# New lists for the order of each engine's instructions in a linear attention and gated FFN kernel

## The chip, the cores and the metric

The kernel runs on one core of a Trainium2 chip. The metric is the device time of one execution in microseconds (us), the median of three runs. A smaller time is better. The engines are TensorE (PE), VectorE (DVE), ScalarE (ACT), GpSimd (POOL) and SyncE (SP); SP computes nothing here and issues every DMA of the kernel.

## The reference

Batch and heads are 8 each, the sequence has 576 positions, the head dimension is 64. The attention is linear; its output, with the heads side by side, is a matrix of 4608 tokens by 512, which goes through a gated feed-forward layer with 1536 inner columns.

```python
q_s = softmax over head_dim of q;  k_s = softmax over seq of k
kv  = np.einsum('bhsd,bhse->bhde', k_s, v)
x   = np.einsum('bhsd,bhde->bhse', q_s, kv)     # then 4608 x 512
a = x @ w_a;  b = x @ w_b                       # 512 x 1536 each
out = (a * b) @ w_out                           # 1536 x 512
```

The inputs are float32, the weights arrive as 64-bit words that the kernel turns into float32 itself.

## The kernel before

The 4608 tokens are worked off in nine chunks of 512. Chunk 0 is done in a start-up part while the weights are being converted; chunks 1 to 8 follow one loop. For each chunk there are six pairs of inner blocks. A pair needs seven products of an input operand (`xo`) with a combination of weights (`ws`), by a scheme with seven instead of eight block products; their results go to the PSUM tiles `kx`, `ky`, `ka` and `kp`. Every operand is kept as a high and a low part, and a product is 12 matmuls of 128x256 (`product`, L839). DVE and ACT combine the results, multiply a by b, and split the outcome into the parts `left`. From chunk 3 on the second layer is done by block products as well (`block_step`, L1478, tiles `po`): each item of six matmuls takes a `left` and a right operand, which is either held in SBUF (`kept`) or loaded (`xo<-dr`) into a ring of two `xo` tiles with two places each. In chunks 1 and 2 the second layer is plain (`project`, L859).

The weights' combinations don't fit in SBUF. They lie in DRAM (`dw`) and each is loaded again for every pair and chunk, 512 KB a time, into one of eight `ws` buffers (L482); the right operands come from `dr`, 256 KB a time (L1416). A load can be issued when the last matmul that reads the buffer's earlier content is done. The attention of the next chunk is spread between the pairs: keys and values are loaded (`kt`, `vt`), `kv_sums` (L588) multiplies them with weights of 64 columns into `pk`, ten matmuls for each pair of heads, and `x_product` (L770) makes the tile `px` from the turned queries. The queries' row statistics go to DRAM (`dq`) and come back spread over partitions (`mr<-dq`, L724, then DVE L731 and ACT L732).

The order of each engine's instructions isn't left to the scheduler. The table `ORDER` has, for each of the five engines, a list of places in the program's own order; `in_order` chains the instructions of that engine by it, and a program builds the semaphores from the data that they pass on. Each engine then works through its list strictly from front to back:

```python
for run in places.split():
    first, _, last = run.partition("-")
    chain += found[int(first):int(last or first) + 1]
for before, ins in zip(chain, chain[1:]):
    tc.add_manual_dep(ins, before.name, ...)
```

SP's list is at the same time the order of the DMA queue: a transfer that waits for its buffer holds up the issue of all that stand behind it.

Of the kernel before, what the change touches and what calls it, by code (L numbers as in the profile page):

```python
# [236 lines left out]
    ),  # L237
    "Pool": (
        "1 4 3 2 5-11 13 12 14 16 15 18 17 19 21 20 22-23 25-26 24 27-29 0 30 32 31 34 33 35 37 36 38-50 "
        "52-54 51 55-58 60-63 59 64-83 "  # L240
    ),
# [1504 lines left out]
```

## Time and profile before

| what | value |
|---|---|
| median of three runs | 957.57 us (955.74, 957.57, 962.2) |
| profiled execution | 960.79 us, its span 959.0 us |
| PE busy | 923.8 us, 96% of the span, 7109 records |
| DVE, ACT, POOL busy | 726.8, 482.1, 101.4 us |
| granted TensorE clock, mean | 0.999 |
| DMA | 308.50 MB, mean 322 GB/s |

The span runs from the first to the last instruction, and what lies around it is 1.8 us. A float32 matmul (L588 and the transposes) shows as two or more records. Matmuls overlap in PE: a record lasts longer than the distance to the next one's start, so a full PE is told by the distance of starts and not by busy time.

### The profile page before, as it was taken

Reading aid. Unit: us, or ns where it says so; the run is one execution under the profiler, and the core shown is the slowest. Engines: PE = TensorE matmul, PEld = TensorE weight load, DVE = VectorE, ACT = ScalarE, POOL = GpSimd, SP = SyncE. Lnnn points to the kernel's source line nnn. Section 1 sums busy time; section 2 is a strip of 40 time slices with the busy share of each in tenths; the row PEclk is TensorE's granted clock in tenths of the full one; section 3 lists DMA queues with packets and bytes.
Section 4 is the critical chain, followed back from the end, with each engine's and each line's share of the span. In section 5 each row is a group of like instructions: output and inputs, shape, how many; then the busy total and the mean of one; then the engine's idle time right before and its main releaser. Section 6 shows DMA issues by size and latency. Waiting matters only on the chain.

```text
span 959.0 us, 19492 instructions
## 1 busy us (share of the span) xinstructions
PE 923.8 (96%) x7109; PEld 846.1 (88%) x7109; DVE 726.8 (76%) x1572; ACT 482.1 (50%) x1346; POOL 101.4 (11%) x88
## 2 busy tenths in 40 slices
PE   6999999999999999989999999899999999999997
PEld 4666768988888999989999998899999999999996
DVE  7867879787897797669868886688868775876456
ACT  8968746433451446535645464345643564343331
POOL 1545351420000000000000000000000000000000
PEclk9999999999999999999999999999999999999999
DMA  9999889899999999998999899996999699957972
GB/s 356 366 384 413 327 296 344 308 325 356 341 405 330 322 384 346 341 302 330 334 319 346 315 329 341 272 384 231 326 319 378 229 364 296 367 184 262 356 255 83
DMA packets 126463, 308.50 MB, mean 322 GB/s; under 512 B 13600, under 2 KB 31648, under 8 KB 126368
## 3 DMA queue, kind: packets, MB, share of 16 engines
q1 hardware_dynamic: 126368, 307.25, 89.9%
q8 instruction: 57, 0.93, 0.4%
q14 instruction: 38, 0.31, 0.1%
HBM read 256.87 MB, written 48.23 MB: 318 GB/s over the span
## 4 chain that ended last, share of the span: by engine, by line
PE 63%; DMA 21%; SPq 3%; DVE 3%; ACT 2%; issue 2%; POOL 2%; DVEq 0%; POOLq 0%; ACTq 0%
PE kx L839 18%; PE po L1478 14%; PE ky L839 9%; PE ka L839 7%; DMA ws<-dw 5%; DMA mr<-dq 5%; DMA xo<-dr 5%; PE po L859 4%; PE pt L814 3%; PE kp L839 3%; PE pk L588 2%; PE po L849 2%; PE px L770 1%; DMA kt<-in_k 1%; SPq L724 1%
## 5 line engine op out<-in xcount | busy, mean ns | idle before, releaser
L839 PE MATMUL kx<-xo,ws 128*128 128x256 f32 x2016 | 277.1, 283 | 4.2 <-DMA ws<-dw 2.9
L839 PEld LDWEIGHTS kx<-xo,ws 128*128 128x128 f32 x2016 | 254.8, 188 | 9.2 <-issue 3.9
L1431 ACT CAST left<-cc 128x256 fp32r<-128x256 f32 x245 | 92.2, 404 | 110.7 <-DVE cc L1447 36.6
L839 PE MATMUL ky<-xo,ws 128*128 128x256 f32 x1008 | 138.8, 283 | 1.3 <-DMA ws<-dw 1.3
L1432 DVE TENSOR_TENSOR left<-cc,left 128x256 fp32r<-128x256 f32 x245 | 97.0, 419 | 46.4 <-ACT left L1431 45.3
L839 PEld LDWEIGHTS ky<-xo,ws 128*128 128x128 f32 x1008 | 127.9, 188 | 3.0 <-issue 1.6
L1478 PE MATMUL po<-xo,left 128*128 128x256 f32 x750 | 108.8, 284 | 6.1 <-DMA xo<-dr 5.4
L1478 PEld LDWEIGHTS po<-xo,left 128*128 128x128 f32 x750 | 96.8, 189 | 8.6 <-issue 4.7
L1478 PE MATMUL po<-kept,left 128*128 128x256 f32 x720 | 103.5, 283 | 0.2 <-ACT acc L1485 0.2
L839 PE MATMUL ka<-xo,ws 128*128 128x256 f32 x720 | 100.4, 283 | 2.3 <-DMA ws<-dw 2.1
L839 PEld LDWEIGHTS ka<-xo,ws 128*128 128x128 f32 x720 | 92.4, 188 | 4.6 <-issue 1.6
L1478 PEld LDWEIGHTS po<-kept,left 128*128 128x128 f32 x720 | 93.3, 189 | 1.5 <-ACT acc L1485 0.4
L681 ACT ACTIVATE qt<-qt,st 128x64 f32<-128x64 f32 x224 | 75.5, 339 | 17.5 <-DVE st L678 14.9
L814 PE MATMUL pt<-xo,ws 128*128 128x512 f32 x288 | 82.9, 427 | 1.1 <-ACT ga L821 1.1
L814 PEld LDWEIGHTS pt<-xo,ws 128*128 128x128 f32 x288 | 52.6, 188 | 23.2 <-issue 9.5
L518 POOL PARTITION_ALL_REDUCE mx<-m x20 | 15.1, 753 | 456.1 <-DVE m L529 443.9
L859 PE MATMUL po<-wo_w,gh 128*128 128x512 f32 x192 | 57.1, 397 | 0.3 <-ACT gh L350 0.3
L1447 DVE TENSOR_TENSOR cc<-cc 128x256 f32<-128x256 f32 x140 | 56.1, 419 | 1.6
L1630 DVE TENSOR_TENSOR cc<-ky,u 128x512 f32<-128x512 f32 x36 | 24.7, 687 | 26.7 <-ACT u L1629 24.4
L681 ACT ACTIVATION_READ_ACCUMULATOR qt<-qt,st 128x1 f32 x224 | 42.1, 188 | 0.0
L839 PE MATMUL kp<-xo,ws 128*128 128x256 f32 x288 | 40.5, 283 | 0.0
L381 POOL TENSOR_TENSOR wr<-raw,wr 128x512 int32<-128x512 int32 x24 | 34.6, 1444 | 55.6 <-DVE raw L378 33.9
(184 smaller groups left out, 1397.3 us busy)
## 6 DMA issues: line engine op xcount, KB each, us to landing
ws<-dw SPq DMA_DIRECT2D x277, 512.0 KB, 6.7
xo<-dr SPq DMA_DIRECT2D x125, 256.0 KB, 5.2
dw<-ws SPq DMA_DIRECT2D x42, 512.0 KB, 6.4
mr<-dq SPq DMA_DIRECT2D x112, 128.0 KB, 6.0
raw<-in_w_ab SPq DMA_DIRECT2D x24, 512.0 KB, 7.7
vt<-in_v SPq DMA_DIRECT2D x28, 325.0 KB, 6.4
qt<-in_q SPq DMA_DIRECT2D x32, 256.0 KB, 5.7
kt<-in_k SPq DMA_DIRECT2D x24, 320.0 KB, 5.8
```

The source lines that it names most:

```text
L381: nc.gpsimd.tensor_tensor(out=r, in0=u, in1=r, op=ALU.add)
L588: nc.tensor.matmul(pk[h * D:(h + 1) * D], kt[:, j, h], vt[:, j, h], start=(j == 0), stop=(j == J - 1),)
L681: nc.scalar.activation(out=qt[:, j, h], in_=qt[:, j, h], func=AF.Exp, bias=st[:, h, 0, j:j + 1], accum_out=st[:, h, 1, j:j + 1],)
L814: nc.tensor.matmul(pt, w[:, wp], x[g][:, xp], start=(g == 0 and i == 0), stop=(g == NP - 1 and i == 2),)
L839: ins = nc.tensor.matmul(pt[:, n], w[:, n, wp, c], x[:, xp, c], start=(first and n == 0 and i == 0), stop=(i == 5), skip_group_check=True,)
L849: nc.tensor.matmul(po[t], g[:, t * P:(t + 1) * P], wo_first[f], start=(f == 0), stop=(f == NF - 1),)
L859: nc.tensor.matmul(po[t], a[:, ts], wo[f][:, w], start=(f == 0 and i == 0), stop=(f == NF - 1 and i == 2),)
L1431: nc.scalar.copy(out=a[:, 0], in_=cc[:, n, part])
L1432: nc.vector.tensor_tensor(out=a[:, 1], in0=cc[:, n, part], in1=a[:, 0].bitcast(F32), op=ALU.subtract)
L1447: nc.vector.tensor_tensor(out=o, in0=x, in1=y, op=op)
L1478: nc.tensor.matmul(pt[:, t], x.left[:, ap, t * P:(t + 1) * P], w[:, wp], start=(first and t == 0 and n == 0), stop=(n == 2), skip_group_ch ...
L1630: nc.vector.tensor_tensor(out=cc[:, 3], in0=ky, in1=u4, op=ALU.add)
```

## The change

Only the table `ORDER` is changed: all five lists are replaced. The instructions themselves, their operands and their buffers are the same; the new table is seven lines longer, so every line number below it grows by 7 (L839 becomes L846, L588 becomes L595, L482 becomes L489). The words given with the change are that the lists come from a longer search that counts mean landing times and changes of weight width. Two lines of the diff, the starts of PE's list:

```diff
-        "4 0-3 5-15 30-33 16-29 34-42 44-47 43 49 60-63 50-55 48 56-59 80-82 64-73 86-89 74-76 90-91 "
+        "0-9 30-33 20-29 10-19 38-41 34-37 42-43 60-63 48 44-47 50-59 49 80-82 64-76 86-89 83-85 90 "
```

The first place is PE where chunk 2 passes into chunk 3. `pk` is the sum of keys times values with weights of 64 columns, `ka`, `kx` and `ky` are first-layer products, `po` belongs to the second layer. Before:

```order
L839 MATMUL kx_4146<-xo_3961,ws_4266 128x256 x12
L588 MATMUL pk_4347<-vt_4157,kt_4155 64x65 x6
L839 MATMUL ka_4436<-xo_4018,ws_4564 128x256 x6
L859 MATMUL po3_3009<-wo11_w_1425,gl1_4142 128x512
L588 MATMUL pk_4347<-vt_4157,kt_4155 64x65 x4
L588 MATMUL pk_4347<-vt_4161,kt_4159 64x65 x6
L839 MATMUL kx_4146<-xo_4025,ws_4378 128x256 x12
L588 MATMUL pk_4347<-vt_4161,kt_4159 64x65 x4
L839 MATMUL ky_4147<-xo_4021,ws_4394 128x256 x6
```

After, the second half of the same `pk`:

```order
L866 MATMUL po1_3007<-wo11_w_1425,gl1_4142 128x512
L866 MATMUL po3_3009<-wo11_w_1425,gl1_4142 128x512
L846 MATMUL kx_4146<-xo_4025,ws_4378 128x256 x12
L595 MATMUL pk_4347<-vt_4161,kt_4159 64x65 x10
L846 MATMUL ky_4147<-xo_4021,ws_4394 128x256 x6
L846 MATMUL kx_4434<-xo_3949,ws_4461 128x256 x12
L846 MATMUL ky_4147<-xo_4021,ws_4394 128x256 x6
```

The ten matmuls of each pair of heads stood in two pieces each, and now stand as one; in PE's whole list the runs of L588's matmuls go from 42 to 28, their 320 matmuls are the same. The first half of this `pk` now stands 25 rows further forward.

The second place is SP's list in chunk 5, ahead of the load `ws_7726`; `mr` are the statistics of the queries, `xo` right operands, `out` a store of results. Before:

```order
L724 DMA mr0_7443<-dq6_7274 64x1x512
L1416 DMA xo_4328<-dr12_3508 128x512
L1416 DMA xo_4328<-dr04_3279 128x512
L1416 DMA xo_4329<-dr21_3705 128x512
L724 DMA mr0_7443<-dq6_7274 64x1x512
L1416 DMA xo_4329<-dr22_3707 128x512
L724 DMA mr1_7444<-dq6_7274 64x1x512
L724 DMA mr0_7449<-dq6_7274 64x1x512
L1463 DMA out_0<-acc_6264 128x2x256
L724 DMA mr0_7449<-dq6_7274 64x1x512
L482 DMA ws_7726<-dw31_2265 128x1024
L482 DMA ws_7760<-dw34_830 128x1024
```

After:

```order
L1470 DMA out_0<-acc_6264 128x2x256
L731 DMA mr1_7450<-dq6_7274 64x1x512
L489 DMA ws_7679<-dw30_816 128x1024
L489 DMA ws_7703<-dw33_2328 128x1024
L719 DMA qtt_7543<-in_q_late 128x512
L489 DMA ws_7726<-dw31_2265 128x1024
L489 DMA ws_7760<-dw34_830 128x1024
```

Between the load `ws_7703`, which stood two rows above the first piece, and `ws_7726` there were eleven transfers, and now there is one; the right operands and most of the statistics have moved ahead of or behind the row of weights.

## Rows read from the trace of the kernel before

**Rows 1.** Page, part 3: DMA queue; packets, MB, share of 16 engines.
```profile
q1 hardware_dynamic: 126368, 307.25, 89.9%
```

**Rows 2.** Windows: us, busy time (instructions) by engine, PEclk, DMA share, GB/s.
```profile
400.00:440.00 40.00, 37.19 (x305) 36.23 (x304) 27.26 (x59) 14.78 (x32) 0.00 (x0) 1.00 1.00 332
...
560.00:640.00 80.00, 73.94 (x646) 71.33 (x645) 57.65 (x134) 37.17 (x112) 1.43 (x2) 1.00 0.97 334
...
840.00:880.00 40.00, 40.00 (x339) 39.98 (x338) 28.27 (x60) 14.60 (x34) 0.00 (x0) 1.00 0.59 209
...
sum 959.00, PE 923.78 PEld 846.12 DVE 726.75 ACT 482.11 POOL 101.35; mean PE 92.38 PEld 84.61 DVE 72.68 ACT 48.21 POOL 10.14
```

**Rows 3.** Waits of PE, whole span: us in total, times, longest.
```profile
PE po L1478 <- DMA xo<-dr: 5.4, 7, 1.5
PE pkb L1115 <- ACT kt_first L1109: 5.4, 1, 5.4
PE kx L839 <- DMA ws<-dw: 2.9, 2, 2.6
PE ka L839 <- DMA ws<-dw: 2.1, 2, 1.2
PE px L770 <- DVE xf L953: 1.8, 1, 1.8
PE px L770 <- ACT qh L350: 1.8, 1, 1.8
...
PE ky L839 <- DMA ws<-dw: 1.3, 1, 1.3
...
PE kx L839 <- ACT u L1564: 0.7, 1, 0.7
```

**Rows 4.** Timeline of PE, dense stretch: start us, us, engine, line, form, count.
```profile
841.78 1.59 PE L839 MATMUL kx<-xo,ws 128*128 128x256 f32 x12
843.21 0.88 PE L1478 MATMUL po<-xo,left 128*128 128x256 f32 x6
```

**Rows 5.** Timeline of PE at 363.6 to 370, around L588's weights of 64.
```profile
366.15 1.69 PE L839 MATMUL kx<-xo,ws 128*128 128x256 f32 x12
367.77 0.45 PE L588 MATMUL pk<-vt,kt 128*64 128x65 f32 x8
368.15 0.98 PE L839 MATMUL ky<-xo,ws 128*128 128x256 f32 x6
368.97 0.87 PE L1478 MATMUL po<-xo,left 128*128 128x256 f32 x6
```

**Rows 6.** Timeline of PE at 603 to 613; in brackets idle time before, releaser.
```profile
607.12 0.88 PE L1478 MATMUL po<-xo,left 128*128 128x256 f32 x6
610.62 1.67 PE L839 MATMUL kx<-xo,ws 128*128 128x256 f32 x12 [2.62 <-DMA ws<-dw]
```

**Rows 7.** Timeline of SP, the DMA queue's issuer, at 593 to 613.
```profile
593.72 6.08 SPq L1416 DMA_DIRECT2D xo<-dr  x3
...
603.53 1.12 SPq L482 DMA_DIRECT2D ws<-dw  x2
```

**Rows 8.** Page, part 6: DMA issues, count, KB each, median us to landing.
```profile
ws<-dw SPq DMA_DIRECT2D x277, 512.0 KB, 6.7
xo<-dr SPq DMA_DIRECT2D x125, 256.0 KB, 5.2
```

**Rows 9.** Chain that ended last, in order of time: start us, us, what.
```profile
228.41 6.86 DMA mr<-dq
...
810.00 5.68 DMA mr<-dq
```

**Rows 10.** Timeline of the end, 950 to 959, PE and DVE.
```profile
952.13 0.87 PE L1478 MATMUL po<-kept,left 128*128 128x256 f32 x6
...
953.66 0.69 DVE L1516 TENSOR_TENSOR acc<-acc 128x512 f32<-128x512 f32 x1
954.38 1.42 DVE L1688 TENSOR_TENSOR acc<-pl,acc 128x256 f32<-128x256 f32 x4
```

More of the change, by code (lines that the diff above doesn't have):

```diff
@@ L31 @@
     "PE": (
[89 rows of a table removed]
[96 rows of a table added]
     ),
     "Activation": (
[44 rows of a table removed]
[44 rows of a table added]
     ),
     "DVE": (
[68 rows of a table removed]
[69 rows of a table added]
     ),
     "Pool": (
-        "1 4 3 2 5-11 13 12 14 16 15 18 17 19 21 20 22-23 25-26 24 27-29 0 30 32 31 34 33 35 37 36 38-50 "
-        "52-54 51 55-58 60-63 59 64-83 "
+        "1 3 2 4-11 13-14 12 16-17 15 18-23 0 25 24 26-50 52-53 51 54-58 60-61 59 62-83 "
     ),
     "SP": (
[34 rows of a table removed]
[34 rows of a table added]
     ),
```

476 rows, old and new, of the table ORDER are left out of this document.

## The prediction

> **What bounds the kernel now.** I read the windows first. PE is busy in 923.78 of 959.00 us, DVE in 726.75, ACT in 482.11 [rows 2], so PE is the bound and what can be won is the time in which it stands still or works badly. Then the dense stretch: a matmul of 128x256 lasts 283 ns in the page, but twelve of them start at 841.78 and the next six at 843.21 [rows 4], so one takes 1.43 / 12 = 0.119 us of PE's time, and the end of a record lies 0.16 us behind the start of the next. So a wait costs about 0.16 us more than the idle time in front of it. From 840 to 880 PE has no idle time at all, and there the DMA engines are busy for 0.59; in 400 to 440 and 560 to 640, where PE is idle for 2.8 and 6.1 us, they are busy for 1.00 and 0.97 [rows 2]. PE loses time where the transfers are dense.
>
> Then the waits of PE, by releaser. Loads of `xo` and `ws` account for 5.4 + 2.9 + 2.1 + 1.3 = 11.7 us in twelve waits [rows 3]. Two waits of 1.8 us at `px` are put down to DVE and ACT, but the chain leads to the transfers of the queries' statistics, with 6.86 us issued at 228.41 and 5.68 us issued at 810.00 [rows 9]. With 0.16 for each of the fourteen waits that makes 11.7 + 3.6 + 2.2 = 17.5 us of waiting for transfers. The start-up takes 5.4 us before the first matmul [rows 3]. What is left of the idle time are some twenty shorter waits for ACT and DVE; the one of 0.7 us for `u` stands for them [rows 3].
>
> **The change, term by term.** No instruction is added or removed, so every term is a wait or a turn of PE that appears or goes.
>
> *Fewer changes of weight width.* The matmuls of L588 have weights of 64 columns, all their neighbours 128. In [rows 5], twelve matmuls of `kx` that stand behind one such run and ahead of another take 367.77 - 366.15 = 1.62 us in place of 1.43, which is 0.19 for going into one run and coming out of one; the six of `ky` that follow a run take 368.97 - 368.15 = 0.82 in place of 0.71, so 0.11 of it is the coming out. The last record of a run may also hold PE longer than those inside it: the eight records take 0.38 us, which would be at most another 0.12 for the run's end. One run costs 0.19 to 0.31 us, and I take 0.25, the middle. The lists have 42 runs before and 28 after, so 14 x 0.25 = 3.5 us go (2.7 to 4.3). Nothing hides this: it is PE's own time, in the engine that bounds.
>
> The Trainium skill, "TensorEngine Tiling (Array Packing)", Key Properties, says that a change of the tiling mode drains TensorE. By that rule each change would cost what one matmul has left when the next would start, 0.16 us by [rows 4], two a run, so 14 x 2 x 0.16 = 4.5 us in place of 3.5, and the forecast would be 947.7. The row, with 0.19 and more for a run, agrees that it costs, and lies a little below the rule.
>
> *Loads that come in time.* For each load of `ws` and `xo` behind the start-up I counted in the lists how much PE work lies between the last matmul that must be done before SP can issue it (through its own buffer, or through one that stands ahead of it in SP's list) and its first reader, at 0.119 us a matmul of 256 columns and in proportion for others. A load takes 6.7 or 5.2 us to land [rows 8], so leads below some 9 us are the tight ones. Before, 18 of `ws` and 23 of `xo` are below 9 us, and 5 and 12 of these below 7; after, 8 and 19, and 0 and 9. Setting the waits of the trace beside the leads of before, the 18 short ones of `ws` hold 5.3 us of the idle time, the 23 of `xo` 3.9, and the other 336 loads the remaining 2.5 to 3. In proportion to the counts, 5.3 x 8 / 18 = 2.4 and 3.9 x 19 / 23 = 3.2 stay, so 3.6 us go, and with 0.16 for five waits fewer 4.4.
>
> The longest of these waits shows what is meant. PE stops for 2.62 us ahead of 610.62 for a load of `ws` [rows 6], which SP issued at 603.53, after having stood for 6.08 us at three loads of `xo` from 593.72 on [rows 7]. In the list before, eleven transfers lie between the load `ws_7703` and this one, after it one; its lead goes from 7.7 to 9.0 us, and that of the next late one, `ws_7843`, from 8.4 to 15.3. For the statistics, the leads in front of the second place of `px` grow from 12 to 16 us to 17 to 22, but those at the first stay at 5.3 for one of two tiles. I let one of the two waits go, 1.8 + 0.16 = 2.0. Together 6.4 us go. The bounds: nothing goes, since the DMA engines have as much to move as before; or all but a fifth of the 17.5 goes, 14 us.
>
> *New tight handovers.* The new lists have 17 places at which only one group of matmuls (up to 1.35 us of work) stands between a product and a reader that needs the result of DVE or ACT, and the old ones 12. The one of which the wait is in [rows 3] is 0.7 us (`kx` for `u`). Five more at half of that, with 0.16 on top, cost 5 x 0.5 = 2.5; some of them sit where the other engine is free, so I take 1.5 (0 to 3). Here DVE's and ACT's next casts are queued behind the late one, and PE's next six or twelve matmuls wait.
>
> *The end and the start.* After its last six matmuls, which start at 952.13, DVE still does one sum over 512 columns and four over 256, up to 955.80 [rows 10]. In the new list nine matmuls of L1682 stand behind the last `po`, so the copy and the sum by ACT and DVE lie beside them, while DVE has one more short sum to do: 0.5 us go (0 to 1). In the start-up ACT does eight short exponentials before the second `kt_first` where it did six, but a transpose of the queries moves forward into the gap; I put it at 0 (1.5 either way).
>
> **Sum.** -3.5 - 6.4 + 1.5 - 0.5 = -8.9 us. The profiled execution took 960.79, its span and 1.8 us around it, and is 3.2 above the median of 957.57. The sum is the same for both: 951.9 for a profiled one, and against the median 957.57 - 8.9 = 948.7.
>
> **Rivals.**
>
> *The waits nearly all go.* If the landing times that the lists count with are those of the chip, most short leads are safe, also the many between 7 and 9 us. Then 14 in place of 6.4 go: 957.57 - 16.5 = 941.1. For it speaks that no `ws` lead is below 7 us any more; against it that nine `xo` leads still are, where the load takes 5.2 at the median and some longer.
>
> *The transfers are the bound in the dense stretches.* The bytes stay the same, 307.25 MB at 89.9% of all sixteen engines [rows 1], and where PE waits they are at 0.97 to 1.00 [rows 2]. Then a load that is issued sooner also lands slower, the other loads move back, and what PE wins at L588 in such a stretch it waits for the next load. Only the width in the rest of the span and the end remain, about 4 us: 953.5. Against it speaks that the stretch from 840 to 880 has room [rows 2], and that in the old list the load at 610.62 was late by its place and not by its 7 us of landing. The Trainium skill, "Perfetto Trace Analysis", What "DMA-bound" means, calls a kernel bound by DMA when the sixteen engines are. By that rule this case would hold through most of the span, as the shares bear out in those two windows alone.
>
> *Slower: SP's list stands still.* SP issues in order, and a transfer moved forward that waits for its buffer holds all that follow. The trace has this once at full size: 6.08 us for three issues [rows 7], and behind it waits of 2.62 [rows 6] and 1.3 [rows 3] at `ws`, 4.2 us with what the idle time leaves out. If the new list has such a place at four more of the chunks from 3 on, 16.8 us come, the 6.4 don't go, and the rest is -2.5: 957.57 - 2.5 + 16.8 = 971.9. It decides from one such place on (4.2 against 2.5). For it speaks that loads of `ws` now stand in rows of three and four with right operands behind them; against it that the count of leads takes in every row ahead in SP's list and still comes out longer.
>
> **How the numbers follow.** About 1% (9.6 us, so 948.0 and 967.1) is what a measurement of this kernel tells from no change; the three runs lie within 0.7%. The forecast has a chance of 0.5, and with the bounds of its terms it runs from 945 to 953, a little under half of it below 948.0. The first rival has 0.2, the second 0.2, the third 0.1, of which 0.07 is above 967.1. Faster by over 1%: 0.23 + 0.2 = 0.43. Slower by over 1%: 0.07. Within: 0.5. The range goes from 940 to 957; it leaves out the third rival and the lower part of the first.
>
> **What would show it.** In the trace after, twelve matmuls beside a run of L595 should still take 1.62 us, and there should be 28 runs. PE's waits for `xo` and `ws` should fall from 11.7 us to about 7.5, and those with `ws` should be the ones that go; the wait at `kx_7660` should be under 1 us. New short waits for DVE or ACT should add up to one or two us. If waits for transfers stay near 12 us at other places, the second rival has it; if SP shows several stops of 4 us and more ahead of waits at `ws`, the third. The forecast is wrong if the leads don't decide which loads are late, so that a count of them says nothing.

## The result and the profile after

The kernel after takes 936.26 us (median of four runs, 933.51 to 936.7), the kernel before 959.26 in the same set (955.74 to 962.2). The ratio is 0.9756, with a 95% interval of 0.9714 to 0.9797; a second set gave 934.95 us and 0.9732 (0.9706 to 0.9758). The change makes the kernel 2.4% faster. The forecast was 948.7 with a range from 940 to 957, so the time lies below the range.

The page of the profiled execution (936.7 us, span 934.9): busy time by engine, the DMA queue, and the shares of the chain that ended last.

```profile
PE 912.5 (98%) x7109; PEld 843.2 (90%) x7109; DVE 724.4 (77%) x1572; ACT 479.7 (51%) x1346; POOL 102.8 (11%) x88
...
q1 hardware_dynamic: 126368, 307.25, 92.6%
...
PE 83%; DMA 9%; DVE 5%; SPq 1%; ACT 1%; issue 1%; DVEq 0%; ACTq 0%
```

The last of these lines on the page of the kernel before:

```profile
PE 63%; DMA 21%; SPq 3%; DVE 3%; ACT 2%; issue 2%; POOL 2%; DVEq 0%; POOLq 0%; ACTq 0%
```

The chain that ended last now leads through PE for 83% of the span and through transfers for 9%; before it was 63% and 21%. The same 307.25 MB are moved as in [rows 1], in less time. PE is idle for 934.9 - 912.5 = 22.4 us; before it was 959.0 - 923.78 = 35.2 [rows 2]. The same windows as in [rows 2]:

```profile
400.00:440.00 40.00, 40.00 (x339) 40.00 (x338) 32.30 (x69) 19.01 (x41) 0.76 (x1) 1.00 1.03 356
560.00:640.00 80.00, 78.03 (x674) 77.25 (x673) 63.07 (x151) 37.53 (x100) 2.19 (x3) 1.00 0.97 343
840.00:880.00 40.00, 40.00 (x340) 40.00 (x339) 24.63 (x54) 13.20 (x30) 0.00 (x0) 1.00 0.94 335
```

In 400 to 440 the DMA engines are as busy as before (1.03, that of before is 1.00), and PE, which stood for 2.8 us, doesn't stand at all. The waits of PE over the whole span, with us in total, times and longest, answer to [rows 3]:

```profile
PE pka L1122 <- ACT kt_first L1116: 7.8, 2, 5.6
PE ky L846 <- DVE cc L1605: 1.8, 1, 1.8
PE po L1485 <- DVE acc L1515: 1.5, 1, 1.5
PE kx L846 <- ACT u L1636: 1.5, 1, 1.5
...
PE po L1485 <- DMA xo<-dr: 0.9, 1, 0.9
PE kx L846 <- DMA ws<-dw: 0.5, 1, 0.5
PE ky L846 <- DMA ws<-dw: 0.5, 1, 0.5
```

Of twelve waits for loads with 11.7 us three with 1.9 are left. The second place of `px` waits for nothing any more (before 3.9 us in three waits, 1.8 + 1.8 of them in [rows 3]). The waits for DVE and ACT behind the start-up are 5.4 us in six, before 5.5 in thirteen. Only the start-up waits longer, 9.4 in place of 7.7 us.

DVE too had stood for transfers, which the prediction doesn't speak of. The view of the waits of DVE, the line of the sum with the queries' statistics, in the kernel before:

```profile
DVE qtt L731 <- DMA mr<-dq: 15.2, 8, 2.7
```

And in the kernel after:

```profile
DVE qtt L738 <- DMA mr<-dq: 1.6, 3, 0.7
```

The timeline of PE around a run of L595 in the kernel after answers to [rows 5]:

```profile
551.39 0.87 PE L1485 MATMUL po<-xo,left 128*128 128x256 f32 x6
552.19 0.80 PE L595 MATMUL pk<-vt,kt 128*64 128x65 f32 x20
552.92 1.70 PE L846 MATMUL kx<-xo,ws 128*128 128x256 f32 x12
554.46 1.60 PE L846 MATMUL ky<-xo,ws 128*128 128x256 f32 x12
```

Six matmuls of `po` ahead of the run take 0.80 in place of 0.71 us, and the twelve of `kx` behind it 554.46 - 552.92 = 1.54 in place of 1.43. So going in costs 0.09 us and coming out 0.11, and what is lost inside the run comes on top.

The timeline of SP at the place of [rows 7]:

```profile
593.90 0.33 SPq L1423 DMA_DIRECT2D xo<-dr  x1
595.13 4.04 SPq L731 DMA_DIRECT2D mr<-dq  x4
599.73 1.69 SPq L489 DMA_DIRECT2D ws<-dw  x2
```

Where three `xo` held SP for 6.08 us, one `xo` takes 0.33 and four loads of `mr` take 4.04, and two loads of `ws` are out by 601.42; the first ones of [rows 7] were issued at 603.53.

The end, PE and DVE, as in [rows 10]:

```profile
927.77 1.78 PE L1689 MATMUL pl<-xo 128*128 128x512 f32 x7
...
929.08 0.68 DVE L1523 TENSOR_TENSOR acc<-acc 128x512 f32<-128x512 f32 x1
929.68 1.74 DVE L1695 TENSOR_TENSOR acc<-pl,acc 128x256 f32<-128x256 f32 x5
```

From the start of PE's last matmul to the end of the span it was 6.29 us and is 5.77.

**Where the time went.** The distance from each PE start to the next, set against the dense rate (869.0 us in both traces), leaves an excess of 78.4 us before and 54.8 after. Distances in front of which PE waited for `ws` or `xo` hold 14.5 us of it before and 2.4 after (-12.1); those at the second place of `px` 4.4 and 0 (-4.4, with 0.16 for each wait); the other waits for DVE and ACT lose 1.2, the start-up gains 1.7. Distances without a wait at or beside a matmul of L588 hold 18.4 and 14.4 (-4.0). The rest is 3.6 us less. Most of it lies in distances that are over 0.1 us too long and yet show no wait: 199 of them with 37.2 us before, 165 with 33.4 after. What held PE there isn't shown. Together with the end (-0.5) that is the 24.1 us between the two profiled executions.

### The profile page after: what moved, and what is told of

Its sections match the earlier page's. It is cut to its first block, busy times and chain, and to the rows that moved or that the text cites. A ratio compares the mean times of both kernels' runs of the same rounds, so it can differ in the third digit from the quotient of the medians.

```text
span 934.9 us, 19502 instructions
## 1 busy us (share of the span) xinstructions
PE 912.5 (98%) x7109; PEld 843.2 (90%) x7109; DVE 724.4 (77%) x1572; ACT 479.7 (51%) x1346; POOL 102.8 (11%) x88
## 3 DMA queue, kind: packets, MB, share of 16 engines
q1 hardware_dynamic: 126368, 307.25, 92.6%
## 4 chain that ended last, share of the span: by engine, by line
PE 83%; DMA 9%; DVE 5%; SPq 1%; ACT 1%; issue 1%; DVEq 0%; ACTq 0%
PE kx L846 22%; PE po L1485 15%; PE ky L846 11%; PE ka L846 8%; PE pt L821 7%; PE po L866 7%; PE po L856 4%; PE kp L846 3%; DMA ws<-dw 3%; PE px L777 2%; PE pk L595 2%; DMA dq<-sst 1%; DMA mr<-dq 1%; DMA xo<-dr 1%; DMA dr<-xo 1%
## 5 line engine op out<-in xcount | busy, mean ns | idle before, releaser
L846 PE MATMUL kx<-xo,ws 128*128 128x256 f32 x2016 | 274.9, 283 | 2.0 <-ACT u L1636 1.5
L846 PEld LDWEIGHTS kx<-xo,ws 128*128 128x128 f32 x2016 | 254.8, 188 | 5.8 <-ACT u L1636 1.7
L846 PE MATMUL ky<-xo,ws 128*128 128x256 f32 x1008 | 139.2, 283 | 2.4 <-DVE cc L1605 1.8
L846 PEld LDWEIGHTS ky<-xo,ws 128*128 128x128 f32 x1008 | 128.0, 189 | 5.0 <-DVE cc L1605 3.1
L1485 PE MATMUL po<-xo,left 128*128 128x256 f32 x750 | 106.7, 282 | 2.6 <-DVE acc L1515 1.5
L1485 PE MATMUL po<-kept,left 128*128 128x256 f32 x720 | 101.1, 282 | 0.0
L846 PE MATMUL ka<-xo,ws 128*128 128x256 f32 x720 | 100.8, 283 | 0.0
L846 PEld LDWEIGHTS ka<-xo,ws 128*128 128x128 f32 x720 | 93.0, 188 | 2.6 <-issue 0.5
L1636 ACT COPY u<-kx 128x512 f32<-128x512 f32 x36 | 21.1, 587 | 65.2 <-PE kx L846 40.3
```

Source lines behind the costliest of these rows:

```text
L846: ins = nc.tensor.matmul(pt[:, n], w[:, n, wp, c], x[:, xp, c], start=(first and n == 0 and i == 0), stop=(i == 5), skip_group_check=True,)
L1485: nc.tensor.matmul(pt[:, t], x.left[:, ap, t * P:(t + 1) * P], w[:, wp], start=(first and t == 0 and n == 0), stop=(n == 2), skip_group_ch ...
L1636: nc.scalar.copy(out=u4, in_=kx)
```

## The experiments

In what follows "over after" and "below before" are differences of ratios, times 960 us; the kernel after counts with 0.9756 for a_pkmore and with 0.9744, the mean of its two sets, for a_late and a_dve. Diffs of lists show rows of the engine named.

### Weight width

**b_pk28**: the kernel before; in PE's list alone the pieces of a `pk` are joined where nothing hinders it, 30 runs in place of 42. One of the twelve places in the table:

```diff
-1994-1999 2093-2098 1993 2000-2009
+2093-2098 1993-2003
```

> The kernel before with PE's list changed at the runs of L588 alone: the pieces of each ten are brought together ahead of the last piece, 42 runs become 30. Theory one, a run costs 0.25 us of PE's own time (0.19 to 0.31): 12 x 0.25 = 3.0 us less (2.3 to 3.7). The rule that each change drains TensorE: 12 x 0.32 = 3.8 us less. Rival, that what PE wins there it waits for at the next load, since the loads set its pace: 0 to 1.5 us less, and the waits for xo and ws grow from 11.7 us to 13 or 14.

Measured: 959.4 us, ratio 0.9976 (0.9953 to 1.0), 2.3 us below before (0 to 4.5), so a gain is not told from none by the times alone. In its trace the distances at L588 lose 18.4 - 14.7 = 3.7 us, which is 0.31 a run; waits for DVE and ACT come back in part. So the width alone is the small part of the gain.

**a_pkmore**: the kernel after with 61 runs in place of 28, each `pk` cut into pieces between the products that follow it.

```diff
-1281-1300 1386-1391 1380-1385
+1281-1284 1291-1294 1386-1391 1295-1297 1285-1287 1380-1385
```

> The kernel after with the tens of L595 from chunk 2 on cut into two or three pieces by the neighbouring groups of six or twelve, 28 runs become 61; all else as in the kernel after (936.3). At 0.25 us a run (0.19 to 0.31): 33 x 0.25 = 8.3 us more (6.3 to 10.2), 944.6. By the rule of a drain at each change, 0.32 a run: 10.6 more, 946.9. Rival, that the runs' length and not their number costs: no change, 936.

Measured: 949.96 us, ratio 0.989 (0.9854 to 0.9927), 12.9 us over after. Its timeline of PE at one place:

```profile
569.94 0.45 PE L599 MATMUL pk<-vt,kt 128*64 128x65 f32 x6
570.31 0.98 PE L850 MATMUL kx<-xo,ws 128*128 128x256 f32 x6
571.23 0.45 PE L599 MATMUL pk<-vt,kt 128*64 128x65 f32 x8
571.61 0.98 PE L850 MATMUL kx<-xo,ws 128*128 128x256 f32 x6
```

Six matmuls of `kx` between two runs take 571.23 - 570.31 = 0.92 us in place of 0.71. Its span is 16.2 us longer than that of after, of which 3.3 are waits (seven more, 2.2 us of idle time); 12.9 / 33 = 0.39 us a run, if all that is left is the runs'. That is over the bounds of both prices, but the time has some 5 us of uncertainty either way.

### Are the transfers the bound?

**b_half**: the kernel before; each load of `ws` brings one half of the bytes, and the products use that half for both blocks of the output, so that half of the weights of each combination take no part. Lists and matmuls stay.

```diff
-        last_w["load"] = nc.sync.dma_start(out=w.bitcast(F32), in_=dw[i, op].bitcast(F32))
+        last_w["load"] = nc.sync.dma_start(out=w[:, 0].bitcast(F32), in_=dw[i, op][:, 0].bitcast(F32))
...
-                        pt[:, n], w[:, n, wp, c], x[:, xp, c],
+                        pt[:, n], w[:, 0, wp, c], x[:, xp, c],
```

> The kernel before with half the bytes in each load of ws (256 in place of 512 KB, the same number of transfers in the same order); the products use the first half of the weights' columns for both halves, so the second half of the inner columns is not computed from its own weights. Same instructions on PE. This is the time with hardly a late load. Theory one and two alike expect landing times of ws near 4 us and a time 13 to 18 us below before, 941 to 946, if landing is what makes the loads late. If SP's stops for PE, DVE and ACT alone are to blame, 6 us or less are won.

Measured: 941.01 us, ratio 0.9791 (0.975 to 0.9832), 20.1 us below before with the lists of before. Its page, the loads with KB and median landing:

```profile
ws<-dw SPq DMA_DIRECT2D x277, 256.0 KB, 4.4
xo<-dr SPq DMA_DIRECT2D x125, 256.0 KB, 3.8
...
mr<-dq SPq DMA_DIRECT2D x112, 128.0 KB, 4.7
```

All loads land sooner, also those whose size is the same (`xo` 3.8 in place of 5.2 [rows 8], `mr` 4.7 in place of 6.0). PE's waits for loads fall to 0.5 us, those at `px` to 0.9, and DVE's for `mr` to 1.5. So transfers of full size had cost the kernel before some 20 us; with some 4 us of width that is as much as the change brings. That it is the same time is shown only by the next run.

**a_half**: the same edit on the kernel after.

> The kernel after with half the bytes in each load of ws, as in b_half; the second half of the inner columns is not computed from its own weights. What transfers still cost the kernel after: its waits for xo and ws (1.9 us) and those for ACT and DVE that go back to a late transfer (2 to 3): 2 to 5 us less than the kernel after, 930 to 933. It then lies 8 to 11 us below b_half (941.0), which is the width (14 runs at 0.37, 5.2) and the rest of the new order. If transfers are as much in the way as before, 10 us or more.

Measured: 935.46 us, ratio 0.9734 (0.9703 to 0.9766), the same as the kernel after (0.9756 and 0.9732). No load is waited for. A quarter of the bytes can go and little or nothing is won, so the rate of the transfers doesn't bound the kernel after, which runs at 92.6% of the sixteen engines and at 1.03 in the window above. How little is less sure than the median says: the four executions take 928.86 us at a granted clock of 0.999, 934.09 at 0.997 and 936.84 and 936.9 at 0.993, so a few us for fewer bytes, as expected, aren't ruled out.

Taken together, the four kernels show what the lists do. With all the bytes the new lists bring 24.6 us (1 less 0.9744), with half of those of `ws` only 5.5 (0.9791 less 0.9734, some 5 either way). So about 19 us of the gain are there only while the loads are of full size: that part is time which late transfers cost, and what is left is about the width.

**a_cap6**: the kernel after; each transfer in SP's list waits in addition for the one six places ahead of it to land. By the program it waits for the one eight places ahead at 818 of 850, and in no trace are there more than eight on the way.

```diff
+    if engine == mybir.EngineType.SP:
+        for before, ins in zip(chain, chain[6:]):
+            tc.add_manual_dep(ins, before.name, ...)
```

> The kernel after, with each transfer made to wait for the landing of the one six places ahead of it in SP's list in place of eight; lists, bytes and all else the same. Theory one, the hold of SP by the transfer eight places ahead is what makes loads late: loads then issue later, the waits for xo and ws come back (1.9 us to 10 or more), and the time is 8 to 30 us longer than the kernel after. Theory two, the DMA engines' rate is the bound: six transfers in flight keep the sixteen engines as busy as eight, each lands sooner by the same share, and the time stays within 4 us of the kernel after.

Measured: 942.15 us, ratio 0.9809 (0.9779 to 0.984), 7.2 us over the kernel after in the same set (934.95). That lies between the two theories. The loads of `ws` land in 5.9 us in place of 6.4 (the line of its page is below), but SP stands longer for the landing of earlier ones; DVE's waits for `mr` rise from 1.6 to 10.2 us, PE's for DVE and ACT from 5.4 to 8.4.

```profile
ws<-dw SPq DMA_DIRECT2D x277, 512.0 KB, 5.9
```

### Mending the kernel before, one list at a time

**b_sp**: the kernel before; in SP's list 13 loads on which PE waited move one to eight rows forward. One of them:

```diff
 L1416 DMA xo_4328<-dr12_3508 128x512
+L482 DMA ws_7726<-dw31_2265 128x1024
 L1416 DMA xo_4328<-dr04_3279 128x512
...
 L724 DMA mr0_7449<-dq6_7274 64x1x512
-L482 DMA ws_7726<-dw31_2265 128x1024
```

> The kernel before with SP's list alone changed: 13 of the 16 loads of ws and xo that came late in its trace are moved ahead by 1 to 8 rows. They hold 11.9 us of PE's idle time, 14 with 0.16 for each. Theory one, place and delay of the issue decide: 8 to 12 us less, since some loads that are pushed back become late; 947 to 951, and the waits for xo and ws fall from 11.7 to 2 to 5 us. Theory two, the DMA engines are the bound in the dense stretches: a load that goes ahead makes another one late, within 3 us of the kernel before, and the waits stay at 9 to 13 us.

Measured: 954.61 us, ratio 0.9931 (0.9904 to 0.9958), 6.6 us below before, less than expected. Lines of PE's waits:

```profile
PE px L770 <- DVE xf L953: 2.3, 1, 2.3
...
PE px L770 <- ACT qh L350: 1.9, 1, 1.9
PE po L1478 <- DVE left L1432: 1.8, 1, 1.8
```

PE's waits for loads fall from 11.7 to 2.4 us, but those at `px` rise from 3.9 to 6.0 and those for DVE and ACT from 5.5 to 7.9.

**b_sp2**: the same idea with 35 rows of SP's list, none moved more than eight places.

```diff
+L474 DMA dw_1549<-ws 128x1024
 L474 DMA dw_1667<-ws 128x1024
 L491 DMA ws_y<-dy_700 128x512
 L491 DMA ws_y<-dy_712 128x512
-L474 DMA dw_1549<-ws 128x1024
```

> The kernel before with SP's list alone changed, further than in b_sp: 35 rows moved by up to eight places over the whole program, loads and statistics both, each where its issue, its landing and the rule of eight transfers in flight leave it time. PE's, DVE's, ACT's and POOL's lists are as before. If the gain of the kernel after lies in SP's list: 9 to 14 us less than the kernel before, PE's waits for xo, ws and at px from 15.3 to 5 or less. If SP's order is held by when PE's list frees the buffers, and PE's own list must change too: no more than the 6.6 us of b_sp.

Measured: 956.1 us, ratio 0.9964 (0.9942 to 0.9986), 3.5 us below before. Loads still hold 5.9 us of waits.

**b_both**: 31 such rows of SP's list and the 30 runs of b_pk28 (edits as in the two above).

> As b_sp2 (31 rows of SP's list moved), and the runs of L588 in PE's list brought together as in b_pk28, 42 runs to 30. If the two parts add: the gain of b_sp2 and 12 x 0.37 = 4.4 us, 13 to 18 us less than the kernel before, and what still parts it from the kernel after (24 us less) is the order of the rest. If the two overlap, since PE then only waits longer at the loads: no more than b_sp2.

Measured: 955.09 us, ratio 0.9942 (0.9917 to 0.9967), 5.6 us below before, a third of what was expected.

**b_pe**: the kernel before; in PE's list the groups that waited change places with the group behind, 16 of them.

```diff
-L839 MATMUL kx_4906<-xo_4025,ws_5073 128x256 x12
 L1478 MATMUL po3_4476<-kept31_3906,left_4414 128x256 x6
+L839 MATMUL kx_4906<-xo_4025,ws_5073 128x256 x12
```

> The kernel before with PE's list alone changed: at 16 of the 18 waits of PE for a late load of ws or xo, or at px, the waiting group of six or twelve matmuls changes places with the group behind it, so that its load has 0.3 to 1.4 us more. SP's list and all others as before. If slack between landing and reader is what decides, whichever list gives it: the smaller of wait and group at each place, some 8 us with 0.16 for the waits that vanish, less 2 or 3 for groups that become late in turn: 5 to 8 us less than the kernel before. If PE's order matters only where it frees buffers: within 2 us.

Measured: 958.59 us, ratio 0.9986 (0.997 to 1.0002), no change. The waits for loads fall to 1.3 us, those for DVE and ACT rise to 11.2.

**b_all**: b_sp, b_pe and the 30 runs together.

> The kernel before with SP's list of b_sp (13 loads forward), PE's list of b_pe and the runs of L588 brought together (42 to 30). If the three are separate gains: 6.6 for b_sp, about 6 for b_pe of which a third meets the same loads, 12 x 0.37 = 4.4 for the width, 13 to 16 us less than the kernel before. If they overlap because both lists mend the same late loads and the next late thing takes the place of each: 8 to 10.

Measured: 958.92 us, ratio 0.9984 (0.9961 to 1.0007), no change. There is no wait for a load in it, but 13.8 us for DVE and ACT and 4.2 at `px`. This fell against my theory, by which the waits of PE for loads were what could be won. Part of the waits that come in their place:

```profile
PE ka L838 <- DVE cc L1622: 1.9, 2, 1.1
PE po L1477 <- DVE acc L1486: 1.9, 1, 1.9
PE px L769 <- DVE xf L952: 1.7, 2, 1.2
```

### The margins of the kernel after

**a_late**: the kernel after; 44 loads of `ws` and `xo` that land less than 2 us ahead of their reader move one or two rows back in SP's list.

```diff
 L489 DMA ws<-dw_1128 128x1024
+L731 DMA mr_4782<-dq_4544 64x1x512 x2
 L489 DMA ws<-dw_2615 128x1024
-L731 DMA mr_4782<-dq_4544 64x1x512 x2
```

> The kernel after with 44 loads of ws and xo that landed less than 2 us ahead of their reader moved back in SP's list by one or two rows (1.9 us later on average); PE's list and all others as after. If the gain of the kernel after is a margin of one or two us at these loads: by their slack in its trace 20 of them come late, 33 us in sum if none relieves another, so 10 to 25 us more than the kernel after (935), most of its gain lost. If PE's new order alone makes the loads safe: within 3 us.

Measured: 952.05 us, ratio 0.9915 (0.9883 to 0.9946), 16.4 us over after. PE's waits for loads are back, 16.0 us in place of 1.9:

```profile
PE kx L846 <- DMA ws<-dw: 9.7, 3, 4.6
...
PE ka L846 <- DMA ws<-dw: 3.5, 2, 2.4
PE po L1485 <- DMA xo<-dr: 2.4, 4, 1.3
```

So one or two places in SP's list, at these 44 loads, decide over two thirds of the gain. By distances of PE's starts, 15.2 of the 18.8 us between the spans stand ahead of loads, and 2.9 in stretches in which PE's granted clock is 0.5 (see the last section).

**a_0, a_best, a_sp2, a_start**: the kernel after once more, and three tries to better it. a_best moves eight rows of the lists of DVE, ACT and SP at the waits that were left, a_sp2 19 rows of SP's list, a_start three at the start-up; one row of each:

```diff
+L489 DMA ws_6401<-dw22_2101 128x1024
 L1423 DMA xo_4328<-dr31_3894 128x512
 L731 DMA mr1_6072<-dq5_5897 64x1x512
...
-L489 DMA ws_6401<-dw22_2101 128x1024
```

```diff
+L473 DMA dy_712<-wy 128x512
 L473 DMA dy_814<-wy 128x512
...
-L473 DMA dy_712<-wy 128x512
```

```diff
+L566 DMA kt_first_79<-in_kt 128x640
 L659 DMA qts<-in_q 128x512
 L345 DMA ident<-in_eye 128x128
 L566 DMA kt_first_81<-in_kt 128x640
-L566 DMA kt_first_79<-in_kt 128x640
```

> The kernel after as it is, so that the three others of this set can be held against it: 0.976 of the time before, PE waits of 1.9 us for xo and ws.

> The kernel after with nine rows of its lists moved: DVE's L1605, L1606 and L1515 ahead of the work they stand behind, L685 behind L1631, ACT's L1636 ahead of four exponentials, and the three late loads of ws and xo 6, 6 and 8 rows forward in SP's list. The waits aimed at are 1.84, 1.45 and part of 1.51 us for DVE and ACT, 0.93, 0.53 and 0.45 for loads, 6.2 with 0.16 for six waits: 4 to 7 us less than the kernel after if a wait removed is time won, 929 to 932. If each is replaced by the next late thing behind it: within 2 us.

> The kernel after with 19 rows of SP's list moved by up to eight places in the same way. PE's transfer waits there are 1.9 us, and some of its waits for ACT and DVE (5.4 us) go back to late transfers of kt and qt: 0 to 5 us less than the kernel after (935). If the order of transfers is as good as it can be, within 2 us.

> The kernel after with three rows of the start-up moved: the load of the second kt_first goes from the fifth to the second place in SP's list, and ACT does its exponential and the copy of the first pka after five of the eight short exponentials. PE's wait of 2.2 us at the second pka should fall to about 1; the time falls by 1 us if PE's next steps follow (0 to 2), and not at all if ACT, which is busy without a break from 4.7 to 16 us, sets the pace of the start-up.

Measured: a_0 934.95 us (0.9732), a_best 936.23 (0.9746, 0.972 to 0.9773), a_sp2 937.14 (0.977, 0.975 to 0.9789), a_start 937.31 (0.9776, 0.9737 to 0.9815). None is better than the kernel after. In a_best most of the waits aimed at are gone and one that wasn't there stands in their place; in a_start the identity for the transposes, moved one place back, lands too late. Its wait, and that of a_best, in the views of PE's waits:

```profile
PE pka L1122 <- DMA ident<-in_eye: 6.1, 1, 6.1
```

```profile
PE po L1485 <- DVE left L1439: 1.8, 1, 1.8
```

### Late statistics and DVE

In the kernels that gain, DVE stands little for `mr` behind the start-up: 1.6 us in the kernel after, 2.9 in a_0, 1.5 in b_half. In those that were mended it stands for 15.7 (b_sp), 10.7 (b_sp2), 11.8 (b_both), 11.6 (b_pe) and 13.9 (b_all). DVE too works through its list in order, so whatever stands behind the sum with the statistics comes late. The rule has exceptions: b_pk28 has 10.6 us of such stops, and a_best has 6.3 and is as fast as a_0 within the interval. Three runs test it.

**b_dve**: the kernel before; seven rows that waited for `mr`, six sums of L731 and one row of ACT's, move two to five rows back.

```diff
-L731 TENSOR_TENSOR qtt<-qtt,mr_6150 128x512
 L1630 TENSOR_TENSOR cc<-ky,u_6415 128x512
 L1631 TENSOR_TENSOR cc<-cc 128x256
 L953 TENSOR_TENSOR xf<-px,mr_6066 128x512
+L731 TENSOR_TENSOR qtt<-qtt,mr_6150 128x512
```

> The kernel before; only the lists of DVE and ACT differ, in seven places: the sum of a turned query tile with its statistics (L731), at which DVE stood for the landing of mr, moves two to five rows back, so that casts and sums that need nothing of it fill the time in which DVE stood. In the kernel before DVE stands for 15.2 us in eight such waits, in the kernel after for 1.6 in three, in the kernel before with half-size loads for 1.5 in two. Theory 1: late statistics stop DVE, the results behind come late, and that is what gave back the gain wherever loads were mended one by one. Then DVE's waits at L731 fall below 5 us, PE's waits for DVE and ACT fall by 2 to 3 us from 5.5 and the time by 2 to 4 us. Theory 2: DVE has room enough (busy three quarters of the span), and its stops cost PE nothing: DVE's waits fall as well, the time stays within 1.5 us.

Measured: 965.94 us, ratio 1.0056 (1.0034 to 1.0077), 5.4 us slower than before, which neither theory expected. DVE's waits for `mr` do fall, from 15.2 to 5.5 us. But PE's for DVE and ACT rise from 5.5 to 9.4 and those at `px` from 3.9 to 5.5, while those for loads fall to 7.0. The costliest place in the timeline of PE:

```profile
821.96 1.19 PE L770 MATMUL px<-qhl,kvh 128*128 128x512 f32 x2 [2.69 <-DVE xf L953]
```

The sums that moved back are themselves on the way to `px`: there two of them run one behind the other at 817.88, and `px` stands for what follows them. PE's waits in sum rise by only 0.8 us. What comes on top stands in PE's clock, in the windows and in the timeline of PE:

```profile
821.30:828.00 6.70, 6.04 (x23) 5.62 (x24) 4.36 (x8) 2.48 (x6) 0.00 (x0) 0.50 1.02 391
```

```profile
823.37 2.76 PE L839 MATMUL kx<-xo,ws 128*128 128x256 f32 x12
825.93 1.48 PE L839 MATMUL ky<-xo,ws 128*128 128x256 f32 x6
```

Behind the wait of 2.69 us the granted clock is 0.50, the lower of its two levels (1.2 in place of 2.4 GHz), and twelve `kx` take 825.93 - 823.37 = 2.56 us in place of 1.43. Another such stretch lies behind the wait of 1.8 us at 239.68; the trace of the kernel before has none ahead of its end. By distances of starts the two hold 4.3 of the 5.8 us between the spans, and the start-up 2.0. In the medians their part isn't shown: executions of the kernel before in this set have mean clocks from 0.992 to 1.0 as well. Moving these sums back didn't mend the late statistics.

**b_alld**: b_all, with eight such sums of L731 and one row of ACT's moved back.

> The kernel before with SP's loads moved forward, PE's waiting groups swapped and 30 runs of L588 (as in the run with all three, which gained nothing), and in addition the sums of L731 moved back in DVE's list at the eight places at which DVE stood for mr in that run, and one row of ACT's. Theory 1: DVE's stops for the statistics had taken the gain; PE's waits for DVE and ACT fall from 13.8 to below 9, those at px stay or fall, and the time is 8 to 14 us below the kernel before. Theory 2: it is the same as without that move, 0 to 3 us below the kernel before.

Measured: 962.87 us, ratio 1.0022 (1.0003 to 1.0041), no gain either. DVE's waits for `mr` are 5.3 us, PE's for DVE and ACT 14.9, as without the move.

**a_dve**: the kernel after; eight sums of L738 move four to six rows forward, so that DVE stands for the landing of `mr`.

```diff
+L738 TENSOR_TENSOR qtt<-qtt,mr_6065 128x512
 L1439 TENSOR_TENSOR left<-cc,left 128x256
...
 L1630 TENSOR_TENSOR cc<-ka,u_6064 128x512
-L738 TENSOR_TENSOR qtt<-qtt,mr_6065 128x512
```

> The reverse on the kernel after: eight sums of L738 whose statistics land just in time are moved four to six rows forward in DVE's list, so that DVE stands some 2 us at each for the landing of mr, as in the kernel before; no load, no product and no transfer moves in its list. Theory 1: PE's waits for DVE and ACT (5.4 us) rise by 5 to 10 us, and the time is 5 to 12 us above the kernel after (941 to 948). Theory 2: DVE makes up for its stops; the time rises by less than 2 us.

Measured: 958.18 us, ratio 0.9978 (0.9954 to 1.0001), 22.5 us over after, twice what the first theory expected. The view of the waits of DVE, the sum's line, and two of PE's longest:

```profile
DVE qtt L738 <- DMA mr<-dq: 19.8, 6, 5.0
```

```profile
PE kp L846 <- DVE cc L1586: 4.7, 2, 3.6
PE px L777 <- DVE qhl L360: 3.9, 2, 2.2
```

DVE stands 18.2 us longer for `mr`. PE's waits for loads are 0.2 us; those for DVE and ACT rise from 5.4 to 17.0, those at `px` from 0 to 5.8, 17.4 in sum. So at these eight places a stop of DVE costs PE nearly its full length, although DVE is busy for only 77% of the span of the kernel after. What the kernel loses beyond that is for the most part the clock: by distances of starts 19.3 of the 25.5 us between the spans are at waits for DVE and ACT and at `px`, and 5.9 in stretches at 0.5. All twelve executions have a mean granted clock of 0.989 to 0.993, those of the kernel after 0.998 to 1.0.

## Why the prediction was wrong

The direction was right and most of the gain came from where it was expected, from waits for transfers; but the term that holds them was sized by a rule that the traces don't bear out. Term by term, with what they show:

- **Loads that come in time**: 6.4 us taken with an upper bound of 14, 16.5 measured (12.1 at loads, 4.4 at `px`). This is the step that failed, and with it the choice of the forecast over the first rival. I let the waits go in proportion to the number of leads below 9 us, 41 before and 27 after. A load is late when its lead is used up by the delay of its issue and its landing, and a threshold doesn't say that. Before, the 41 had a mean lead of 7.21 us, an issue delay of 1.03 and a landing of 5.10; those that were late held 9.2 us. After, the 27 have 7.52, 0.61 and 4.94, and one is late by 0.45. Three small shifts in the same direction raise the mean margin from 1.1 to 2.0 us, and the late ones go, while the count only fell by a third. a_late shows how thin that margin is: one or two places back, and 16.4 us return.
- What the leads left out: SP also stops for other engines and for earlier transfers. In the kernel before it stands at a store of the statistics for DVE, in SP's timeline:

```profile
385.30 0.32 SPq L482 DMA_DIRECT2D ws<-dw  x1
391.51 0.61 SPq L696 DMA_DIRECT2D dq<-sst  x1
```

  5.9 us pass there, and five loads behind it came late between 402 and 448 us though their leads were 10 to 15 us. How much of that is this stop's isn't shown, since SP stands for PE there as well. In the new list two of the three late loads have leads of 17 and 18 us, but were issued 11 and 12 us after the last matmul that they had to wait for. So the prediction's own sign of being wrong is met in part: leads alone don't decide which loads are late. Stops of SP are the third rival's mechanism, but in the old list; in the new one I saw none of its size ahead of waits at `ws`, and it did not come.
- **The statistics**: I took them in only through the two waits at `px`. DVE's stops for them, 15.2 us before, were not in the sum. a_dve shows that such stops can cost their length. In b_dve 9.7 us of them went and nothing was won; in b_half, where the transfers land sooner, 1.5 us are left.
- **Fewer changes of width**: 3.5 us taken with bounds of 2.7 and 4.3, 4.0 measured (18.4 to 14.4 us of excess at L588), 0.29 a run. b_pk28 gives 0.31, a_pkmore 0.39, so the price was somewhat low. The rule of the Trainium skill ("TensorEngine Tiling (Array Packing)", Key Properties), worked out as 0.32 a run and 4.5 us, lies among these; a_pkmore with 12.9 us is nearer to the rule's 10.6 than to my 8.3, but its uncertainty covers both.
- **New tight handovers**: 1.5 us taken as a loss, and 1.2 fewer measured. There are six such waits behind the start-up where there were thirteen; the three long ones that are left take 1.5 to 1.8 us.
- **The end** came out as taken, 0.5 us less. **The start-up**, put at 0 and up to 1.5 either way, lost 1.7.
- **No term at all** had the 3.6 us at distances that show no wait; their cause stays open.

From 948.7 to 936.26 are 12.4 us. The terms miss by 10.1 at loads and `px`, 2.7 at handovers, 0.5 of width and the 3.6, less 1.7 of the start-up: 15.2 between the profiled executions. The medians lie 1.1 us closer together than these, and the kernel before took 1.7 us more in this set than the 957.57 that the forecast set out from.

The first rival, that the waits nearly all go, is what happened; its 941.1 is still 4.8 us too much, and whether its reason holds, that the landing times of the search are those of the chip, no run tests. The second falls by a_half: the kernel after keeps the DMA engines as busy as the one before (92.6% and 89.9%), and fewer bytes bring it little or nothing. What was right in it is that in the kernel before the bytes did cost time (b_half), since landings took up the leads.

The signs named beforehand: the waits for `xo` and `ws` were to fall to 7.5 us and fell to 1.9; the wait at `kx_7660` was to be below 1 us, and no wait for a load in the whole span is longer than 0.9; new waits of one to two us for DVE or ACT are there, three of them, but others went. The waits with `ws` were to be the ones that go, but those with `xo` went as far, from 5.4 to 0.9 us. There are 28 runs of L595, and twelve `kx` behind one take 1.54 us; the 1.62 of the prediction are for twelve between two runs.

What stays open: no repair of one list of the kernel before brings more than 6.6 us, and the three together bring nothing. The waits for loads go in them and waits for DVE and ACT come in their place (13.8 us in b_all). Why these come isn't shown: DVE's own stops for `mr` are no longer there than before (13.9 and 15.2 us). That the gain comes from all five lists together is what these runs suggest. It wasn't tried to run one kernel's list of SP with the other's lists of the compute engines, and which rows of those lists are needed isn't shown. How much of the 15.2 us of DVE's stops stood in PE's way in the kernel before isn't shown either.

## What to carry to other kernels

Where every engine works through its list in order, a load is worth its margin at the reader: lead less issue delay less landing, load by load, with the tail and not the count below a threshold. Take in the transfers that the other engines wait for as well, since a stop of an engine with room to spare can be passed on to the one that bounds (a_dve). Repairs of single late loads gave back most of what they won to waits for other engines here (b_sp, b_all). The test for what late transfers cost is to shrink them, in both orders: what a new order still wins with small transfers isn't theirs.

## What the runs showed of the hardware

- PE never stands in 400 to 440 us of the kernel after with the sixteen DMA engines at 1.03, and with a quarter of the bytes gone (a_half) the time of the kernel is the same to within a few us. Here the busy share of the DMA engines didn't tell whether they bound.
- Landing time depends on what else is on the way: `xo`, 256 KB, takes 5.2 us beside 512 KB loads of `ws` and 3.8 beside 256 KB ones. With six in place of eight on the way `ws` lands in 5.9 in place of 6.4 us, and the kernel takes 7.2 us longer; that this comes from later issues is argued, not shown. In the chain of the kernel after SP is held in that way, each transfer being issued when the one ahead has landed (at 686.02 and 693.71):

```profile
678.91 7.11 DMA ws<-dw
...
686.62 7.09 DMA mr<-dq
693.73 6.89 DMA xo<-dr
```

- A change of weight width costs PE about 0.1 us going in and 0.1 coming out, and with what is lost inside the run 0.29 to 0.39 us for each run of 64-column weights among 128-column ones.
- PE's granted clock can fall to 0.5 (1.2 in place of 2.4 GHz) behind a wait of PE. In a_dve, the timeline of PE and the windows behind that wait:

```profile
298.07 0.98 PE L846 MATMUL kp<-xo,ws 128*128 128x256 f32 x6 [3.61 <-DVE cc L1586]
```

```profile
298.90:302.30 3.40, 3.40 (x17) 3.21 (x16) 1.74 (x4) 0.06 (x1) 0.00 (x0) 0.50 0.56 193
```

  Ahead of the last matmuls there are five such stretches in a_dve, two in b_dve and a_late, one in the kernel after (from 279.2 us on, 1.5 us of excess) and none in the kernel before. In each PE has just stood for 1.5 to 4.6 us, or stands. But the kernel before stands 2.62 us ahead of 610.62 [rows 6] without one, so the length of the wait alone doesn't tell whether the clock falls. Where it does, the wait costs more than the 0.16 us beyond its idle time that the prediction reckons with: 1.1 us at the twelve `kx` of b_dve.
